# Attention and two feed-forward stages on one core: how many chunks of the first feed-forward run beside attention

## The chip, the core and the metric

The kernel runs on one core of a Trainium2 chip. What counts is the device time of one execution in microseconds (us). The kernel before took 1000.54 us in the median of three runs (1000.1 to 1000.61). Five engines work side by side: PE (matrix products), DVE and ACT (element work), POOL (element work), and SP, which here only issues transfers. PEld in the profile is PE's loading of stationary operands, which lies beside its products.

## What is computed

Three stages follow one another. Inputs are q, k, v of 4 batches, 8 heads, 576 positions and 64 dimensions; 2304 tokens of 512 features come out.

```
scores = q k^T / sqrt(D) - slope[h] * |i - j|, only where 0 <= i - j < 128
x      = softmax(scores) v            -> [2304, 512]
x      = ((x w_a) * (x w_b)) w_out    # feed-forward 1, hidden width 1536
h      = x w_in                       # feed-forward 2, hidden width 2048
g      = h where h >= 1, 0 where h <= -1, (h + 1)^2 / 4 between
out    = g w_out2                     -> [2304, 512]
```

The weights come as 64-bit floats. Each operand of a product is split into a high and a low part, and three products (high with high, high with low, low with high) stand for one.

## The kernel before, in words

**Tokens and chunks.** The tokens are cut into five blocks, 0 to 4, of 512, 512, 512, 512 and 256 tokens, and blocks 0 to 2 also into six halves of 256. The hidden width of feed-forward 1 is cut into 12 chunks of 128. One chunk takes three weights: a and b (into the hidden width, 12 matmuls each: 4 pieces of the 512 features times 3 products) and o (back to 512 features, 12 matmuls). So a chunk of a block costs 36 matmuls, whose length is the number of tokens, 512 or 256. Feed-forward 2 has 16 chunks of two weights.

**Attention.** The generator `attention()` lists 80 rounds of 128 queries for a pair of heads. Each is one step for the scores (L323 on PE, L329 on DVE, the exponential L333 on ACT, L338 on POOL, L339 on DVE, the division L342 or L344 on ACT or POOL), one for the transposition (L358 on PE, L360 copies it to `pt`), and one for the product with v for several rounds (L379 on PE), after which ACT writes `xh` (L392) and DVE `xl` (L393). That makes 192 steps. In the profile `xh` and copies through a helper stand as L149, copies on DVE as L151, and `xl` as L143.

**Feed-forward 1.** `gate()` runs the products with a and b (L523 to L525), copies a's result with ACT to `a_sb` (L563), multiplies it with b's on DVE (L568), and `parts()` splits it into `gh` (L545, ACT) and `gl` (L143). `down1_half()` (L596, 256 tokens) and `down1()` (L624 to L626) take these to accumulators. Where a half's chunks end, ACT and DVE copy the two accumulators to tiles `y`, and SP stores these in `x2p` in device memory (L607). When the block is taken up again, SP loads these sums back into `xsum` (L618), and later chunks are added to them.

**What sets the order.** `products()` lists turns: six halves with the first `N0` chunks each; then block 3 and block 4 with their first `N0` chunks, which wait for the whole of attention; then, as `TURN1` says, all blocks with chunks `N0` to `N1`; then, as `TURN2` says, with chunks `N1` to 12; then feed-forward 2. A half waits until attention has made its tokens. Every matmul group of three is a yield; at each, the main loop adds `PACE[turn]` to what it owes and takes one attention step per whole unit owed (L753 to L756). So `PACE` is the number of attention steps per three matmuls beside each turn; the last entry holds for all later turns. A scheduler then hoists what is ready, so that the recorded order is near but not equal to that.

**Weights.** `decode()` (L451) loads a weight (L459) and turns it into two 32-bit tiles with ACT, DVE and POOL (L472 to L490; L489 is ACT's last step). There are 15 slots for weights (`WP`) and 2 more once attention has ended (`W2`). A slot comes free when the last turn that uses its weight is recorded. Beside attention 15 weights, five chunks, are decoded.

**Where attention ends.** `step()` closes attention's pools and opens those of the later stage. One of these, tag `t` with two buffers, holds `a_sb`, and `y` of the half that is then under way.

Of the kernel before, what the change touches and what calls it, by code (L numbers as in the profile page):

```python
# [26 lines left out]
def attention_and_two_ffns(  # L27
# [45 lines left out]
    LORD = [['q', 0, 2, 'S'], ['k', 0, 2, 'A'], ['q', 2, 8, 'S'], ['k', 2, 8, 'A'], ['v', 0, 8, 'A']]  # L73
    LT = 3
    LV = 5
    N0 = [4, 5, 5, 5, 5]
    N1 = 9
    NDIAG = 2
    NHALF = 6
    PACE = [0.8, 0.8, 0.5, 0.5, 0.5, 0.5, 0.5, 0.5, 0.3]  # L80
    PT = 5
    PUMP = [2, 0]
    SB = 4
# [409 lines left out]
    def pump():  # L493
        if not waiting:
            return False
        free = [
            s for s in slots if len(s[2]) < s[1] or s[2][0] in retired
        ]
        if not free:
            return False  # L500

        pool, n, held = min(free, key=lambda s: order.index(s[2][0]) if len(s[2]) == s[1] and s[2][0] else -1)
        if len(held) == n:
            held.popleft()
        key = waiting.popleft()
        held.append(key)
        with tc.high_priority() if not later and HP(order.index(key)) else ExitStack():
            decode(key, pool)
        return True
# [170 lines left out]
    def products():  # L680
        behind = deque()

        def run(up, down, i, fs, x, n, final, lag):
# [9 lines left out]
        turns1 = [  # L693
            *((i, range(N0[t0 // TB])) for i, (t0, _) in enumerate(halves[:NHALF])),
            *((i, range(N0[i])) for i in range(NHALF // 2, len(blocks))),
            *((i, range(N0[i], N1)) for i in TURN1),
            *((i, range(N1, NF1)) for i in TURN2),
        ]
# [46 lines left out]
    for need in products():  # L745
        if need is not None:
            begun += 1
            while not later and (need > NT or not ready(need)):
                step()
                steps += 1  # L750
                if steps % PUMP[0] == PUMP[1]:
                    pump()
        owed += PACE[min(begun, len(PACE) - 1)]  # L753
        while owed >= 1.0:
# [32 lines left out]
```

## Time and profile before

| what | value |
|---|---|
| median of three runs | 1000.54 us |
| the profiled execution | 999.14 us, span of its instructions 997.4 us |
| PE busy | 967.6 us, 97% of the span |
| DVE, ACT, POOL busy | 612.7, 407.0, 178.2 us |
| stretch beside attention | 0 to about 245 us |
| TensorE's granted clock | 1.00 throughout |

The span is the time from the first to the last instruction that the profiler saw; 1.74 us of the execution lie around it. A turn's first L523 shows when it starts: the halves of block 0 at 29.0 us, of block 1 at 125.8, of block 2 at 205.7; block 3 at 265.5 and block 4 at 306.5; the turns of `TURN1` from 329.4, the last of them (block 4) at 466.9; block 0 of `TURN2` at 498.4; feed-forward 2 at 595.1. A busy time counts the modelled length of each matmul, and matmuls overlap; the pace of a run of matmuls is read from the distance of their starts.

### The profile page before, as it was taken

The page shows a single profiled execution, that of the slowest core. Times are in us where ns is not written, and L with a number is a line of the kernel's source. Part 1 is how long each engine was busy: PE and PEld are TensorE (multiplying, and loading weights), DVE is VectorE, ACT ScalarE, POOL GpSimd, SP SyncE. Part 2 cuts the span into 40 slices and gives each one's busy share as a digit, 9 for nine tenths or more (in the row PEclk, how much of TensorE's full clock was granted, in tenths as well). Part 3 has the DMA queues.
Part 4 walks back from the last instruction along what each step waited for, and adds up shares of the span by engine and source line. Part 5 has one row for each costly group of instructions (what it writes and reads, how often), then busy time and mean ns, then how long its engine had stood idle before and what let it go on. Part 6 is the DMA issues. An engine that isn't in the chain of part 4 may idle for free.

```text
span 997.4 us, 15119 instructions
## 1 busy us (share of the span) xinstructions
PE 967.6 (97%) x5624; PEld 836.9 (84%) x5624; DVE 612.7 (61%) x1354; ACT 407.0 (41%) x970; POOL 178.2 (18%) x289
## 2 busy tenths in 40 slices
PE   4889999999999999999999999999999999999998
PEld 3678899999989888888988887888888888888887
DVE  6999755553726993223995299634995446644443
ACT  4978767563314441112343245423552223322222
POOL 4777623221101100000222224000020000000001
PEclk9999999999999999999999999999999999999999
DMA  9777442311511331000231012100230000001111
GB/s 195 152 168 141 99 90 53 70 35 52 179 67 43 122 111 43 1 1 1 91 104 60 1 64 77 51 1 1 85 106 21 1 1 22 1 1 43 42 43 64
DMA packets 124121, 62.32 MB, mean 62 GB/s; under 512 B 95760, under 2 KB 116240, under 8 KB 123664
## 3 DMA queue, kind: packets, MB, share of 16 engines
q1 hardware_dynamic: 119824, 60.31, 22.6%
q10 hardware_dynamic: 4224, 1.05, 0.6%
q8 instruction: 44, 0.72, 0.3%
q14 instruction: 29, 0.24, 0.1%
HBM read 53.48 MB, written 7.86 MB: 62 GB/s over the span
## 4 chain that ended last, share of the span: by engine, by line
PE 84%; DVE 7%; DMA 3%; ACT 3%; issue 1%; POOL 1%; SPq 0%; DVEq 0%; ACTq 0%; POOLq 0%
PE mm L523 15%; PE mm L525 15%; PE mm L524 15%; PE acc L662 6%; PE acc L663 6%; PE acc L664 6%; PE acc L596 3%; PE acc L626 3%; PE acc L625 3%; PE acc L624 3%; PE ps_s L323 2%; PE ps_o L379 2%; PE ps_t L358 2%; DMA w<-in_moe_w_b_dram 1%; ACT s L333 1%
## 5 line engine op out<-in xcount | busy, mean ns | idle before, releaser
L523 PE MATMUL mm<-xh,wh 128*128 128x512 f32 (+1 forms) x912 | 321.2, 353 | 1.0 <-DVE c_sb L580 0.8
L525 PE MATMUL mm<-xh,wl 128*128 128x512 f32 (+1 forms) x912 | 314.2, 345 | 0.8 <-POOL wl L143 0.8
L524 PE MATMUL mm<-xl,wh 128*128 128x512 f32 (+1 forms) x912 | 314.5, 345 | 0.1
L523 PEld LDWEIGHTS mm<-xh,wh 128*128 128x128 f32 x912 | 172.2, 189 | 23.7 <-DVE c_sb L580 1.2
L524 PEld LDWEIGHTS mm<-xl,wh 128*128 128x128 f32 x912 | 172.4, 189 | 21.8 <-DVE xl L143 0.4
L525 PEld LDWEIGHTS mm<-xh,wl 128*128 128x128 f32 x912 | 172.1, 189 | 21.7 <-POOL wl L143 1.0
L579 ACT ACTIVATE c_sb<-c_sb,half 128x512 f32<-128x512 f32 (+1 forms) x80 | 54.5, 681 | 167.1 <-DVE c_sb L578 167.1
L662 PE MATMUL acc<-wh,gh 128*128 128x512 f32 x288 | 112.3, 390 | 0.0
L663 PE MATMUL acc<-wl,gh 128*128 128x512 f32 x288 | 112.2, 390 | 0.0
L664 PE MATMUL acc<-wh,gl 128*128 128x512 f32 x288 | 110.4, 390 | 0.0
L568 DVE TENSOR_TENSOR a_sb<-mm,a_sb 128x256 f32<-128x256 f32 (+1 forms) x74 | 40.2, 543 | 113.8 <-PE mm L525 103.5
L578 DVE TENSOR_SCALAR c_sb<-mm 128x512 f32<-128x512 f32 (+1 forms) x80 | 50.8, 635 | 82.5 <-PE mm L525 79.3
L143 POOL TENSOR_TENSOR gl<-c_sb,gh 128x256 fp32r<-128x256 f32 x16 | 14.4, 901 | 386.4 <-ACT gh L545 379.0
L143 POOL TENSOR_TENSOR gl<-a_sb,gh 128x256 fp32r<-128x256 f32 x40 | 36.6, 916 | 247.8 <-ACT gh L545 247.2
L580 DVE SCALAR_TENSOR_TENSOR c_sb<-mm,c_sb 128x512 f32<-128x512 f32 (+1 forms) x80 | 50.7, 635 | 39.0 <-ACT c_sb L579 39.0
L333 ACT ACTIVATE s<-s,nmax 128x192 f32<-128x192 f32 (+2 forms) x144 | 62.1, 433 | 23.9 <-DVE nmax L329 23.4
L563 ACT COPY a_sb<-mm 128x256 f32<-128x256 f32 (+1 forms) x74 | 34.5, 467 | 89.2 <-PE mm L525 81.9
L545 ACT CAST gh<-c_sb 128x512 fp32r<-128x512 f32 (+1 forms) x80 | 46.2, 579 | 55.8 <-DVE c_sb L580 46.2
L489 ACT CAST wh<-e 128x512 fp32r<-128x512 f32 x68 | 42.3, 622 | 64.1 <-DVE e L488 37.1
L472 ACT ACTIVATE e<-w 128x512 f32<-128x512 f32 x65 | 43.8, 674 | 58.5 <-DMA w<-in_moe_w_in_dram 14.2
L545 ACT CAST gh<-a_sb 128x256 fp32r<-128x256 f32 (+1 forms) x74 | 37.2, 502 | 74.3 <-DVE a_sb L568 74.0
L625 PE MATMUL acc<-gl,wh 128*128 128x512 f32 (+1 forms) x184 | 66.2, 362 | 0.2 <-DVE gl L143 0.2
(84 smaller groups left out, 1607.6 us busy)
## 6 DMA issues: line engine op xcount, KB each, us to landing
w<-in_moe_w_out_dram SPq DMA_DIRECT2D x28, 512.0 KB, 3.5
w<-in_moe_w_in_dram SPq DMA_DIRECT2D x16, 512.0 KB, 3.6
w<-in_moe_w_a_dram SPq DMA_DIRECT2D x12, 512.0 KB, 3.9
w<-in_moe_w_b_dram SPq DMA_DIRECT2D x12, 512.0 KB, 3.8
out_dram<-osum SPq DMA_DIRECT2D x18, 256.0 KB, 2.1
qraw<-in_q_dram SPq DMA_DIRECT2D x48, 72.0 KB, 2.7
kraw<-in_k_dram SPq DMA_DIRECT2D x48, 72.0 KB, 2.9
v<-in_v_dram SPq DMA_DIRECT2D x24, 128.0 KB, 2.9
```

Of the source, the lines that this page charges most:

```text
L143: eng.tensor_tensor(out_, a, hi.bitcast(F32), ALU.subtract)
L333: nc.scalar.activation(at(z, i), at(z, i), AF.Exp, bias=nmax[:, z : z + 1], scale=-1.0, accum_out=ssum[:, z : z + 1],)
L523: nc.tensor.matmul(ps, wh[:, cs], xh[:, c], start=(c == 0), stop=False)
L524: nc.tensor.matmul(ps, wh[:, cs], xl[:, c], start=False, stop=False)
L525: nc.tensor.matmul(ps, wl[:, cs], xh[:, c], start=False, stop=(c == NC - 1))
L545: nc.scalar.copy(hi[:, :n], t[:, :n])
L578: nc.vector.tensor_scalar(c_sb[:, :n], ph[:, :n], -1.0, None, ALU.max)
L579: nc.scalar.activation(c_sb[:, :n], c_sb[:, :n], AF.Square, bias=half, scale=0.5)
L625: nc.tensor.matmul(accs[c][:, :n], wh[:, cs], gl, start=False, stop=False)
L662: nc.tensor.matmul(accs[s], gh[:, ss], wh, start=begin, stop=False)
L663: nc.tensor.matmul(accs[s], gh[:, ss], wl, start=False, stop=False)
L664: nc.tensor.matmul(accs[s], gl[:, ss], wh, start=False, stop=end)
```

## The change

Three tables of numbers change, no other line. Every half, block 3 and block 4 take chunks 0 to 2 (`N0`) and no longer 0 to 3 or 0 to 4. `TURN1` takes chunks 3 to 7 of all five blocks (it was 5 to 8, and 4 to 8 for block 0), `TURN2` chunks 8 to 11 (it was 9 to 11). Beside all turns 0.8 attention steps are taken per three feed-forward matmuls; it was 0.8 beside the first two halves, 0.5 beside the next six turns and 0.3 later.

```diff
-    N0 = [4, 5, 5, 5, 5]
-    N1 = 9
+    N0 = [3, 3, 3, 3, 3]
+    N1 = 8
-    PACE = [0.8, 0.8, 0.5, 0.5, 0.5, 0.5, 0.5, 0.5, 0.3]
+    PACE = [0.8]
```

In numbers of the recorded order: matmuls of 512 tokens go from 2856 to 3036, those of 256 tokens from 1632 to 1272, and PE's changes between attention and feed-forward matmuls from 259 to 171. All 15 decodes of the first stage stay beside attention.

**PE, near the middle of the first batch's attention.** `ps_s`, `ps_t` and `ps_o` are attention's scores, transposes and values, `mm` and `acc` feed-forward 1. In a row before:

```order
L379 MATMUL ps_o_1749<-pt_1621,v1_146 64x128 x4
L379 MATMUL ps_o_1749<-pt_1647,v1_146 64x128 x4
L379 MATMUL ps_o_1749<-pt_1687,v1_146 64x64 x4
L323 MATMUL ps_s_1789<-kt_1583,diag0_128 128x64
L323 MATMUL ps_s_1789<-kt_1583,diag0_128 128x128
L358 MATMUL ps_t_1806<-ident_84,s2_138 128x128 x4
L525 MATMUL mm_1802<-xh0_106,wl_582 128x256
L323 MATMUL ps_s_1816<-kt_1583,diag0_128 128x192 x2
L523 MATMUL mm_1802<-xh0_106,wh_581 128x256
L524 MATMUL mm_1802<-xl0_107,wh_581 128x256
L525 MATMUL mm_1802<-xh0_106,wl_582 128x256
L523 MATMUL mm_1802<-xh0_106,wh_581 128x256
```

In a row now, at the same rounds of attention:

```order
L379 MATMUL ps_o_1740<-pt_1689,v1_146 64x64 x4
L323 MATMUL ps_s_1774<-kt_1584,diag0_128 128x64
L323 MATMUL ps_s_1774<-kt_1584,diag0_128 128x128
L358 MATMUL ps_t_1787<-ident_84,s2_138 128x128
L323 MATMUL ps_s_1794<-kt_1584,diag0_128 128x192 x2
L358 MATMUL ps_t_1787<-ident_84,s2_138 128x128 x3
L358 MATMUL ps_t_1807<-ident_84,s3_141 128x128 x4
L379 MATMUL ps_o_1814<-pt_1722,v2_148 64x128 x2
L379 MATMUL ps_o_1814<-pt_1738,v2_148 64x128 x4
L323 MATMUL ps_s_1827<-kt_1584,diag0_128 128x192 x2
L358 MATMUL ps_t_1843<-ident_84,s0_132 128x128 x2
L323 MATMUL ps_s_1851<-kt_1584,diag0_128 128x192 x2
```

Chunk 3 of the half before stood among these rounds (`mm_1802`, with `xh0`); now attention's rounds follow each other. Between `ps_o` of the round before (numbered 1656, now 1661) and that of the rounds after (1939, now 1903) 79 feed-forward matmuls stood in a row before and 12 stand now. Counted from the start to the end of this piece it was 294 and is 240.

**SP, where attention ends.** `xsum` are the loads of block 0's and 1's sums (1 MB each), `y` the store of a half's sums, `w64` weights that were not loaded beside attention. In a row before:

```order
L618 DMA xsum0_4581<-x2p_150 128x2048
L618 DMA xsum1_4891<-x2p_150 128x2048
L459 DMA w64_3672<-in_moe_w_a_dram 128x4x128
L459 DMA w64_3738<-in_moe_w_b_dram 128x4x128
L607 DMA x2p_150<-y_3732 128x512
L607 DMA x2p_150<-y_3735 128x512
```

And now:

```order
L618 DMA xsum0_3921<-x2p_150 128x2048
L618 DMA xsum1_4231<-x2p_150 128x2048
L607 DMA x2p_150<-y_3357 128x512
L607 DMA x2p_150<-y_3360 128x512
L459 DMA w64_3363<-in_moe_w_a_dram 128x4x128
L459 DMA w64_3425<-in_moe_w_b_dram 128x4x128
```

The two stores stood behind two weights, now directly behind the two loads; they belong to the fifth half before the change as after it.

**ACT, at the same place.** `xh4` is attention's last piece of x, `e` and `wh` steps of a decode. In a row before, from the first `a_sb` of the later stage:

```order
L563 COPY a_sb_3700<-mm_3687 128x256
L149 COPY y_3732<-acc_3308 128x512
L545 CAST gh_3716<-a_sb_3700 128x256
L472 ACTIVATE e_3676<-w64_3672 128x512
L472 ACTIVATE e_3742<-w64_3738 128x512
L563 COPY a_sb_3766<-mm_3753 128x256
L563 COPY a_sb_3813<-mm_3800 128x256
```

And now, from the fifth half's `y`:

```order
L149 COPY y_3357<-acc_3029 128x512
L149 CAST xh4_114<-ps_o_3298 128x256
L563 COPY a_sb_3391<-mm_3378 128x256
L563 COPY a_sb_3453<-mm_3440 128x256
L545 CAST gh_3407<-a_sb_3391 128x256
L545 CAST gh_3469<-a_sb_3453 128x256
L472 ACTIVATE e_3367<-w64_3363 128x512
```

Now `y_3357` takes the first of the two buffers of tag `t` in the later stage (its companion `y_3360` on DVE the second), and the next two `a_sb` take the same buffers again. On PE 60 feed-forward matmuls of halves are left behind the last of attention's; it was 195. Of the 60, the order has 12 for `acc_3411` and `acc_3412` (the two accumulators that `y_3357` and `y_3360` empty), 24 for `mm_3378` and `mm_3440`, then matmuls of block 3 (`mm_3485`, which takes the place in PSUM that `mm_3378` held until `a_sb_3391` is copied from it), and the other 24 among these.

## Rows read from the trace of the kernel before

**Rows 1.** The page's part 1: busy us (share of span), instructions.
```profile
PE 967.6 (97%) x5624; PEld 836.9 (84%) x5624; DVE 612.7 (61%) x1354; ACT 407.0 (41%) x970; POOL 178.2 (18%) x289
```

**Rows 2.** Windows: length, busy us (instructions) per engine, granted clock, DMA share, GB/s.
```profile
25.00:100.00 75.00, 66.40 (x568) 57.45 (x567) 71.14 (x233) 63.11 (x208) 57.18 (x85) 1.00 0.75 155
113.70:130.90 17.20, 17.20 (x171) 16.41 (x170) 10.59 (x47) 14.15 (x52) 7.41 (x20) 1.00 0.34 60
130.90:236.60 105.70, 105.70 (x973) 102.11 (x973) 53.34 (x223) 66.77 (x231) 30.71 (x84) 1.00 0.25 55
466.90:498.40 31.50, 31.50 (x253) 31.01 (x252) 28.29 (x54) 12.45 (x26) 6.20 (x6) 1.00 0.23 69
```

**Rows 3.** Timeline of PE, 256 tokens a matmul: start, us, line, operands.
```profile
247.06 0.28 PE L596 MATMUL acc<-gh,wh 128*128 128x256 f32 x1
...
247.66 0.28 PE L596 MATMUL acc<-gh,wl 128*128 128x256 f32 x1
```

**Rows 4.** Timeline of PE, 512 tokens a matmul.
```profile
401.61 0.39 PE L523 MATMUL mm<-xh,wh 128*128 128x512 f32 x1
...
402.75 0.39 PE L525 MATMUL mm<-xh,wl 128*128 128x512 f32 x1
```

**Rows 5.** Timeline of PE, entering feed-forward work from attention work.
```profile
131.33 0.36 PE L523 MATMUL mm<-xh,wh 128*128 128x256 f32 x1
131.53 0.28 PE L524 MATMUL mm<-xl,wh 128*128 128x256 f32 x1
...
132.29 0.41 PE L523 MATMUL mm<-xh,wh 128*128 128x256 f32 x1
132.54 0.28 PE L524 MATMUL mm<-xl,wh 128*128 128x256 f32 x1
```

**Rows 6.** Timeline of DVE at the two ends of the stretch.
```profile
113.67 0.42 DVE L143 TENSOR_TENSOR xl<-ps_o,xh 128x256 fp32r<-128x256 f32 x1
...
130.89 0.36 DVE L143 TENSOR_TENSOR xl<-ps_o,xh 128x192 fp32r<-128x192 f32 x1 [0.94 <-ACT xh L149]
```

**Rows 7.** Groups of ACT, 113.7 to 130.9: busy, mean ns, idle before, releasers.
```profile
L563 ACT COPY a_sb<-mm 128x256 f32<-128x256 f32 x3 | 1.1, 361 | 0.0
L545 ACT CAST gh<-a_sb 128x256 fp32r<-128x256 f32 x2 | 0.8, 388 | 0.0
```

**Rows 8.** Groups of PE, 130.9 to 236.6, one of each three alike.
```profile
L523 PE MATMUL mm<-xh,wh 128*128 128x256 f32 x106 | 35.5, 335 | 0.0
...
L596 PE MATMUL acc<-gh,wh 128*128 128x256 f32 x56 | 18.4, 329 | 0.0
```

**Rows 9.** Groups of ACT, 130.9 to 236.6.
```profile
L545 ACT CAST gh<-a_sb 128x256 fp32r<-128x256 f32 x14 | 5.6, 399 | 3.7 <-DVE a_sb L568 3.7
...
L563 ACT COPY a_sb<-mm 128x256 f32<-128x256 f32 x13 | 4.8, 371 | 3.8 <-PE mm L525 3.4 <-POOL ssum L338 0.3
...
L149 ACT COPY y<-acc 128x512 f32<-128x512 f32 x3 | 1.7, 572 | 0.0
```

**Rows 10.** Timeline of SP's queue where attention ends.
```profile
244.66 0.80 SPq L618 DMA_DIRECT2D xsum<-x2p  x2
248.02 0.38 SPq L459 DMA_DIRECT2D w<-in_moe_w_a_dram  x1
...
251.07 2.28 SPq L607 DMA_DIRECT2D x2p<-y  x2
```

**Rows 11.** DMA issues, whole span: KB each, median us to landing.
```profile
x2p<-y SPq DMA_DIRECT2D x12, 256.0 KB, 2.4
```

**Rows 12.** DMA issues from 244 to 258 us, columns as before.
```profile
xsum<-x2p SPq DMA_DIRECT2D x2, 1024.0 KB, 6.6
...
x2p<-y SPq DMA_DIRECT2D x2, 256.0 KB, 4.5
```

**Rows 13.** The decode's last ACT step, in 305 to 345 us.
```profile
L489 ACT CAST wh<-e x9: 620/622/628, 308.0 to 342.7; 128x512 fp32r<-128x512 f32 x9
```

## The prediction

> **What bounds the kernel now.** I read the page's part 1 first, then busy times by stretch, then timelines of single engines. PE is busy 97% of the span [rows 1], so the time is PE's work plus PE's few holes, and a change counts if it alters one of these. The stretches say where there are holes: from 25 to 100 us PE has 66.40 of 75 us and DVE 71.14; from 113.7 on PE has all of every stretch, at a granted clock of 1.00 in each [rows 2]. So beside attention PE is kept full from about 114 us by feed-forward work. The change takes a third of that work away, and the question is whether what is left still fills the holes.
>
> **Part 1, the matmuls themselves.** Ten half-chunks of 36 matmuls (28 beside attention become 18) leave, and five block-chunks of 36 come: 360 matmuls of 256 tokens for 180 of 512. Starts of the short ones lie 0.60 us apart over five of them, 0.120 us each [rows 3]; of the long ones 1.14 us over five, 0.228 us [rows 4]. 360 x 0.120 = 43.2 us against 180 x 0.228 = 41.0 us: a gain of 2.2 us.
>
> The Trainium skill ("TensorE: Matmul & The Clock Gate", section "Wait — 56ns, not 53.3ns?") speaks against most of it: a warm array starts a matmul every N / 2.4 GHz plus about 2.5 ns. By that the short one takes 109.2 ns and the long one 215.8 ns, both below the trace, and the gain would be 0.5 us, the sum 1.7 us higher.
>
> **Part 2, fewer changes between attention and feed-forward.** PE's order has 259 such changes and will have 171, so 44 entries into feed-forward work go. After an entry the second matmul starts 0.20 and 0.25 us after the first and not 0.12 [rows 5], 0.08 to 0.13 us more: 3.5 to 5.7 us in all. It may be that those starts only wait for attention's matmuls still in the array, which would cost nothing; I bound it by 0 and 5.7 and take the nearer row, 3.5 us gained.
>
> **Part 3, the stretch in which attention runs alone.** Block 0's second half now ends after chunk 2, and the third half cannot begin until attention has made block 1's first tokens. Between the two rounds of attention that end on DVE at 113.67 and 130.89 us [rows 6] PE will have 12 feed-forward matmuls and not 79. Counted to the stretch's end it will have done 240 and not 294: 54 x 0.120 = 6.5 us of PE's work still to do. Against it stands how much sooner the stretch ends. It took 17.2 us; without feed-forward work ACT decides. ACT was busy 14.15 us [rows 2], of which 1.1 + 0.8 us were feed-forward copies [rows 7] and about 0.4 us (one copy) stay: 12.7 us of work. That is the lower bound, if ACT never waits; at ACT's share of the old stretch, 14.15 / 17.2 = 82%, it takes 15.5 us; at worst it stays at 17.2, since the chain scores, DVE, ACT, POOL, DVE, ACT, transposition is as long as before. The loss is 6.5 - (17.2 - 12.7) = 2.0, 6.5 - 1.7 = 4.8, or 6.5 us. I take 4.8, as the share is a row of this very stretch. DVE's 10.59 us of 17.2 leave it behind ACT.
>
> **Part 4, the rest of attention.** From 130.9 to 236.6 us three times 106 and three times 56 [rows 8], 486 of 973 matmuls, are feed-forward. Of the 648 of all halves 240 will be done and 60 come after attention, so 348 remain. PE would need 105.7 - (486 - 348) x 0.120 = 89.1 us. ACT's 66.77 us fall by the copies of the work that goes, 28% of 5.6 + 4.8 + 1.7 us [rows 9], to 63.4, 71% of PE's time. Attention's chain gets shorter distances between its links (0.8 steps per three matmuls and not 0.5). Nothing excludes small holes: 0 to 3 us, I take 0.5, near PE's full row of before. That all of it were covered would mean 0. Were the whole rest to run with PE as in 25 to 100 us (89% busy), it would be 11 us; that is a rival.
>
> **Part 5, where attention ends.** Before, 195 feed-forward matmuls (23 us) stood behind attention's last, now 60 (7 us). At attention's end, call it t, pools change, and in SP's queue come the two 1 MB loads of `xsum`, issued together at 244.66 before [rows 10]. What is issued behind them is late: the store of `y` took 4.5 us to land where its median is 2.4 [rows 11, 12], though 6.4 us lay between the issues, which looks like a queue that hands out its bytes in order (2 MB of sums, 1 MB of weights, 0.5 MB of stores). Before, PE did not notice: 23 us of matmuls were there to do. Now `y_3357` and `y_3360`, copies of the fifth half, need the new pool, so they wait for t, though their sums are long done; `acc_3411`, PE's next matmul, waits for that copy: 0.57 us [rows 9] and the way there and back, 0.95 us together (estimate). Then 36 matmuls are free to run, 4.3 us, to t + 5.3. The next, `mm_3485`, needs `a_sb_3391`, whose buffer is `y_3357`'s, so it waits for the store to land. The store is issued about t + 1.2, behind the sums: these took 6.6 us to land [rows 12], and the store's own bytes come after them, so t + 7.8. ACT's copy, 0.4 us, and the signals follow. PE stands 3.0 us there, then some 0.6 us for the next `a_sb` behind the decodes that pile up on DVE, and 0.4 us while the short sequence drains: with the 0.95, 5.0 us. Bounds: 1.0 if the store overtakes the loads and lands in its median 2.4 us (t + 3.6, before PE needs it); 7 if the store takes two sums and both stores' time.
>
> **Part 6, the two last turns of feed-forward 1.** Five chunks' 15 weights fill the 15 slots, so at the passage from `TURN1` to `TURN2` only two weights of chunk 8 can be ready, and ten more are decoded while block 4 passes through both turns; it was seven. A decode takes (342.7 - 308.0) / 8 = 4.3 us [rows 13], ten 43 us; block 4 has 9 chunks, 324 x 0.120 = 39 us. Before: 8 chunks, 35 us, for 30 us of decodes, and PE was busy 31.50 of 31.50 us, DVE 28.29 [rows 2], with block 0's matmuls hoisted among it. So some 4 us are short and the hoisted block covers most. 0 to 4 us; 1.0, since before the row shows full cover. The passage to feed-forward 2 keeps its lookahead: 0.
>
> **Sum.** - 2.2 - 3.5 + 4.8 + 0.5 + 5.0 + 1.0 = + 5.6 us on the profiled execution's 999.14 us (span 997.4, 1.74 around it), 1004.7. That execution lies 1.40 us below the median of the runs; on the median the forecast is 1006.1, rounded 1006.0 us. With all gains at their largest and costs at their smallest, - 2.2 - 5.7 + 2.0 + 1.0 = - 4.9: 995.6; with the reverse, - 2.2 + 6.5 + 3 + 7 + 4 = + 18: 1018.8.
>
> **Rivals.**
> A, the other side: *the store is not behind the sums.* Place: `mm_3485`. If the store lands within 4.1 us of its issue (t + 1.2 to t + 5.3), PE never waits there and part 5 falls to 1.0; then the decodes alone remain, and with part 3 at ACT's own work, 2.0, the sum is - 2.2 - 3.5 + 2.0 + 0.5 + 1.0 + 1.0 = - 1.2 to - 4.9: about 997 us, faster. For it: sixteen DMA engines share the issues, and the store is only 256 KB. Against it: 4.5 us in the one place where this was seen.
> B, *attention becomes the bound to its end*: + 11 in place of 0.5, 1016 us. For it: 25 to 100 us, where PE is 89% busy beside the same pace of 0.8 steps. Against it: there 15 decodes load DVE to 95%, which are over by 114 us.
> C, *the last weights are late*: part 6's ten decodes are held by DVE, which was busy 90% of that stretch already; three more weights uncovered are 13 us, 1018 us. Against it: PE's full row, and block 0 can be hoisted further.
> D, *TensorE's clock falls at a new hole.* The granted clock was 1.00 in all stretches, those with holes of 11% too [rows 2]. If it fell to 1.2 GHz for 10 us of matmuls at t, these take 20: 1016 us. The same page of the Trainium skill (Part 1, "What's actually happening") has the clock gated down when the array has been idle; no row here shows it.
> E, *nothing happens*: the added holes and the saved matmuls cancel, 1000.5; it is the overlap of A and the forecast.
>
> **Chances.** The forecast, 1001 to 1011, 0.62; A 0.23 with E inside; B 0.07; C 0.05; D 0.03. What a measurement can tell from no change is 0.2%, 2 us: 998.5 to 1002.5. Of the forecast 0.08 lies within it and 0.54 above; of A 0.13 is faster, 0.10 the same; B to D are slower. Faster 0.13, same 0.18, slower 0.69. The range reaches from the middle of A to the start of B, 998.0 to 1013.0; the likeliest case's own is 1001 to 1011.
>
> **What would show it.** In the profile after: PE with holes between the rounds that ended at 113.67 and 130.89, and none from there to t; a wait of PE at L523 for ACT's `a_sb` (L563), about 3 us, some 5 us behind attention's last L379, and one at L596 for ACT's or DVE's `y`; the store of `y` taking over 6 us from issue to landing; PE's busy time lower by a few us. A store landing within 3 us proves A; holes all through 130 to 240 us prove B; a wait at L525 or L626 for `wl` before feed-forward 2 proves C. No new hole over 1 us anywhere would prove the forecast wrong.

## The result: 9 us slower

The changed kernel takes 1009.6 us in the median of its runs (1007.03 to 1010.62), the kernel before 1000.58 us: a ratio of 1.0082 (95% interval 1.0069 to 1.0095). The forecast was 1006.0 us, range 998.0 to 1013.0. The profiled execution took 1009.34 us, span 1007.6, 10.2 us more than before's span.

**Where PE waits now.** The longest sums of PE's waits (engine, line, what it waited for, us in all, times, longest):

```profile
PE ps_q L235 <- DMA qh<-in_q_dram: 9.5, 2, 6.3
PE ps_t L358 <- POOL s L344: 6.4, 7, 2.3
...
PE mm L523 <- ACT a_sb L563: 4.1, 1, 4.1
...
PE acc L596 <- ACT y L149: 1.1, 1, 1.1
```

In the kernel before:

```profile
PE ps_t L358 <- POOL s L344: 4.3, 5, 1.3
...
PE acc L596 <- DVE y L151: 0.6, 1, 0.6
...
PE mm L523 <- ACT a_sb L563: 0.2, 1, 0.2
```

The 4.1 us of `mm` (L523) for `a_sb` are new, and so is the wait of `acc` (L596) for a `y` at attention's end; the 0.6 us before lay at 106 us. By stretch (columns as in [rows 2]; the second is the stretch in which attention runs alone, the third the rest of attention, the fourth what follows the hole at t):

```profile
25.00:100.00 75.00, 68.94 (x587) 59.76 (x586) 70.78 (x226) 61.33 (x201) 56.61 (x83) 1.00 0.76 160
115.69:130.32 14.63, 13.17 (x127) 11.87 (x126) 11.01 (x51) 13.18 (x49) 5.83 (x17) 0.98 0.47 98
130.32:219.00 88.68, 88.68 (x834) 84.65 (x834) 51.23 (x218) 63.51 (x223) 28.00 (x81) 1.00 0.29 59
232.00:236.00 4.00, 3.46 (x9) 2.77 (x10) 2.13 (x5) 2.88 (x6) 1.43 (x2) 0.57 0.70 240
```

The granted clock was 1.00 before; now it is 0.98 in the second row and 0.57 in the fourth. The ends of the stretch on DVE, which answer to [rows 6]:

```profile
115.69 0.42 DVE L143 TENSOR_TENSOR xl<-ps_o,xh 128x256 fp32r<-128x256 f32 x1
...
130.32 0.35 DVE L143 TENSOR_TENSOR xl<-ps_o,xh 128x192 fp32r<-128x192 f32 x1
```

It took 14.6 us, before 17.2. The profile's chain of work through it (what released each step, or the step before it on its engine) runs over PE's own matmuls, but for one piece of 4 us, in which DVE transposes q and k of later rounds (`diag`, `kt`) and copies a `y` before POOL can divide and PE go on:

```profile
117.73 0.68 DVE diag L296
118.41 0.03 issue
118.44 0.78 DVE diag L296
119.22 0.03 issue
119.25 0.78 DVE kt L299
120.03 0.57 DVE y L151
...
120.84 0.43 POOL s L344
121.28 0.04 issue
121.32 0.33 PE ps_t L358
```

ACT does not stand in this chain. Where attention ends, SP's queue and DMA (as [rows 10, 12]):

```profile
222.91 0.82 SPq L618 DMA_DIRECT2D xsum<-x2p  x2
223.81 1.06 SPq L607 DMA_DIRECT2D x2p<-y  x2
```
```profile
xsum<-x2p SPq DMA_DIRECT2D x2, 1024.0 KB, 6.2
x2p<-y SPq DMA_DIRECT2D x2, 256.0 KB, 8.2
```

The store of `y` stood right behind the sums and took 8.2 us to land, before 4.5. ACT shows both waits: `y` is copied right after attention's last `xh`, and the next `a_sb` only when the store has landed:

```profile
222.81 0.21 ACT L149 CAST xh<-ps_o 128x64 fp32r<-128x64 f32 x1 [3.08 <-PE ps_o L379]
223.20 0.58 ACT L149 COPY y<-acc 128x512 f32<-128x512 f32 x1 [0.18 <-ACT xh L149]
...
232.12 0.75 ACT L563 COPY a_sb<-mm 128x256 f32<-128x256 f32 x2 [8.02 <-DMA x2p<-y]
```

PE's timeline there (the bracket is idle time before, and what ended it):

```profile
223.84 0.38 PE L596 MATMUL acc<-gh,wh 128*128 128x256 f32 x1 [1.07 <-ACT y L149]
...
228.13 0.28 PE L525 MATMUL mm<-xh,wl 128*128 128x256 f32 x1
232.54 0.80 PE L523 MATMUL mm<-xh,wh 128*128 128x512 f32 x1 [4.13 <-ACT a_sb L563]
233.13 0.63 PE L524 MATMUL mm<-xl,wh 128*128 128x512 f32 x1
233.56 0.63 PE L525 MATMUL mm<-xh,wl 128*128 128x512 f32 x1
...
235.27 0.56 PE L523 MATMUL mm<-xh,wh 128*128 128x512 f32 x1
235.66 0.39 PE L524 MATMUL mm<-xl,wh 128*128 128x512 f32 x1
235.89 0.40 PE L525 MATMUL mm<-xh,wl 128*128 128x512 f32 x1
```

PE stands for 4.13 us, then come matmuls of 512 tokens at a distance of 0.43 us, and from 235.66 on at 0.23: seven of them take 3.12 us (232.54 to 235.66) where 7 x 0.228 = 1.6 would do, 1.5 us more. That distance is the lower of the two clock levels, 1.2 GHz.

**Account.** At like places of attention I compare the times, and count each feed-forward matmul that is missing as 0.120 us:

| place (`xl` on DVE, where nothing else is said) | now, us | before, us | matmuls done, now / before | late by, us |
|---|---|---|---|---|
| the first | 30.1 | 29.1 | 1 / 1 | 1.1 |
| before the lone stretch | 99.8 | 96.8 | 202 / 164 | -1.6 |
| its start | 115.7 | 113.7 | 228 / 231 | 2.4 |
| its end | 130.3 | 130.9 | 244 / 294 | 5.4 |
| end of attention's last product on PE | 222.8 | 244.5 | 588 / 814 | 5.4 |
| the last | 224.1 | 245.5 | 590 / 821 | 6.4 |

The last `xl` has PE's wait of 1.07 us for `y` already behind it; attention's last product does not.

At equal work still to do, the new kernel is 9.5 us behind from 272 us on to the end of feed-forward 1, and 10.2 us from feed-forward 2's first turns to the end. With the 2.2 us that the longer matmuls save put back, that is: 1.1 at the start, 4.3 up to the end of the lone stretch (1.3 ahead of it, 3.0 in it), nothing in the rest of attention, 6.3 where attention ends, nothing between the two last turns of feed-forward 1, 0.8 at the entry to feed-forward 2, less 2.2 = 10.3. The 1.3 are the balance of a gain of 2.7 us up to 99.8 us, which the forecast did not have, and a loss of 4.0 from there to 115.7, more than half of it one wait of PE for POOL's division (2.3 us, to 111.7).

### The profile page after: what moved, and what is told of

Its sections match the earlier page's. It is cut to its first block, busy times and chain, and to the rows that moved or that the text cites. A ratio compares the mean times of both kernels' runs of the same rounds, so it can differ in the third digit from the quotient of the medians.

```text
span 1007.6 us, 14724 instructions
## 1 busy us (share of the span) xinstructions
PE 971.8 (96%) x5444; PEld 831.8 (83%) x5444; DVE 609.9 (61%) x1354; ACT 405.6 (40%) x960; POOL 170.1 (17%) x279
## 4 chain that ended last, share of the span: by engine, by line
PE 81%; DVE 5%; DMA 3%; issue 1%; ACT 1%; POOL 0%; DVEq 0%; ACTq 0%; SPq 0%; POOLq 0%
PE mm L523 15%; PE mm L524 14%; PE mm L525 14%; PE acc L664 6%; PE acc L663 6%; PE acc L662 6%; PE acc L624 4%; PE acc L625 4%; PE acc L626 4%; PE ps_s L323 3%; PE ps_o L379 2%; PE ps_t L358 2%; PE acc L596 2%; DMA x2p<-y 1%; DVE e L482 1%
## 5 line engine op out<-in xcount | busy, mean ns | idle before, releaser
L523 PE MATMUL mm<-xh,wh 128*128 128x512 f32 (+1 forms) x872 | 309.1, 356 | 4.2 <-ACT a_sb L563 4.1
L523 PEld LDWEIGHTS mm<-xh,wh 128*128 128x128 f32 x872 | 164.8, 189 | 28.1 <-ACT a_sb L563 4.6
L568 DVE TENSOR_TENSOR a_sb<-mm,a_sb 128x512 f32<-128x512 f32 (+1 forms) x69 | 39.3, 571 | 145.8 <-PE mm L525 137.8
L563 ACT COPY a_sb<-mm 128x512 f32<-128x512 f32 (+1 forms) x69 | 33.7, 489 | 108.8 <-PE mm L525 98.8
L625 PE MATMUL acc<-gl,wh 128*128 128x512 f32 (+1 forms) x204 | 73.7, 365 | 0.2 <-DVE gl L143 0.2
L626 PE MATMUL acc<-gh,wl 128*128 128x512 f32 (+1 forms) x204 | 73.5, 364 | 0.0
L545 ACT CAST gh<-a_sb 128x512 fp32r<-128x512 f32 (+1 forms) x69 | 36.3, 526 | 88.6 <-DVE a_sb L568 88.3
L624 PE MATMUL acc<-gh,wh 128*128 128x512 f32 (+1 forms) x204 | 69.9, 365 | 0.0
L143 POOL TENSOR_TENSOR gl<-a_sb,gh 128x256 fp32r<-128x256 f32 x30 | 27.1, 905 | 253.1 <-ACT gh L545 236.3
L323 PE MATMUL ps_s<-kt,diag 128*128 128x192 f32 (+2 forms) x288 | 63.1, 341 | 5.4 <-DVE kt L151 4.6
```

Source lines behind the costliest of these rows:

```text
L323: nc.tensor.matmul(ps[:, z, c : 3 * D], qd[:, i - q0 // D, :], kt[:, (i - 2) * D + c - k0 : (i + 1) * D - k0], start=True, stop=True,)
L523: nc.tensor.matmul(ps, wh[:, cs], xh[:, c], start=(c == 0), stop=False)
L545: nc.scalar.copy(hi[:, :n], t[:, :n])
L624: nc.tensor.matmul(accs[c][:, :n], wh[:, cs], gh, start=begin, stop=False)
L625: nc.tensor.matmul(accs[c][:, :n], wh[:, cs], gl, start=False, stop=False)
L626: nc.tensor.matmul(accs[c][:, :n], wl[:, cs], gh, start=False, stop=end)
```

## Experiments

Each ratio is to the kernel before, run beside it.

**e1: the stores of y on another queue.**
```diff
-                nc.sync.dma_start(
+                (nc.scalar if later else nc.sync).dma_start(
                     x2p[:, i, 2 * z : 2 * z + 2, :], ...
```


> The changed kernel, in which the stores of y that are issued after attention's end go out on ACT's queue and not on SP's behind the two loads of xsum. Theory (PE waited 4.1 us for a buffer whose store lay 8.2 us behind 2 MB of loads, and ran seven matmuls at 1.2 GHz after the hole): the store lands within about 5 us, PE's wait at mm_3485 falls below 1 us and the granted clock stays at 1.00 there; 1009.6 - 4.1 - 1.5 = about 1004, 1003 to 1006. Rival (the bytes are shared by all queues, or the wait is for the change of pools): the store still takes 7 us or more, 1008 to 1010.

1007.22 us, ratio 1.0066 (1.0051 to 1.0081). PE's waits and the DMA issues around t:

```profile
PE mm L523 <- ACT a_sb L563: 3.8, 1, 3.8
PE acc L596 <- ACT y L149: 1.1, 1, 1.1
```
```profile
xsum<-x2p SPq DMA_DIRECT2D x2, 1024.0 KB, 6.6
x2p<-y ACTq DMA_DIRECT2D x2, 256.0 KB, 8.1
```
```profile
228.00:230.00 2.00, 0.00 (x0) 0.00 (x0) 0.00 (x0) 0.00 (x0) 0.00 (x0) 1.00 1.00 387
```

The store was issued at once, on ACT's queue, and landed after 8.1 us all the same; PE waited 3.8 us, and the clock fell again. So it is not SP's order that delays the store. The last row (columns as in [rows 2]) has the DMA engines wholly busy while the store is under way, which speaks for the rival, that they are shared with the loads; that it is the 2 MB of sums, e5 shows. What e1 gained of its 2 us lies mostly ahead of t, where the edit touches nothing: its profiled execution has no fall of the clock at 112 us.

**e5: the loads of the sums later.**
```diff
+                nc.gpsimd.tensor_copy(sums[i][:, 0, 0, :1], g[0][:, :1].bitcast(F32))
                 nc.sync.dma_start(sums[i], x2p[:, 2 * i : 2 * i + nb])
```


> The changed kernel, in which each load of xsum follows a one-column POOL write that needs the first gh of its turn, so that the 2 MB no longer start at attention's end. Theory (PE's wait of 4 us at mm_3485 and the matmuls at 1.2 GHz behind it come from the stores of y sharing the DMA engines with these loads; another queue alone did not help): the store lands in 2 to 4 us, the wait is under 0.5 us, no fall of the clock there; ratio to before falls from 1.0082 by 0.005 to about 1.003, some 1003 to 1005 us. Rival (the wait comes from the change of pools, or is refilled by waits for the next weights): above 1.006.

1002.87 us, ratio 1.0021 (1.0009 to 1.0033). Around t:

```profile
PE acc L596 <- ACT y L149: 1.1, 1, 1.1
```
```profile
x2p<-y SPq DMA_DIRECT2D x2, 256.0 KB, 2.2
```

The store lands in 2.2 us, PE's wait for `a_sb` is gone, and so is the fall of the clock there. That is 0.006 of the 0.0082. By the account, attention's end now costs 0.6 us. The 1.1 us for `y` stay; that `y` waits there for the change of pools is read from the code and was not tested. The 12 runs lie between 999.98 and 1005.41 us, and this spread is not explained.

**e7: the same edit in the kernel before.**


> The kernel before with the loads of xsum later, nothing else. Theory (23 us of matmuls cover the loads there): no difference, ratio 0.999 to 1.001. Rival (the loads cost the kernel before too): 0.995 to 0.998.

999.72 us, ratio 0.9995 (0.9986 to 1.0003): no difference. So the loads became dear only with the change; that the 23 us of matmuls behind attention covered them before fits this.

**e2: block 0's halves keep four chunks.**
```diff
-    N0 = [3, 3, 3, 3, 3]
+    N0 = [4, 3, 3, 3, 3]
```


> The changed kernel with N0 = [4, 3, 3, 3, 3]: block 0's halves keep their fourth chunk, so feed-forward matmuls stand again in the stretch in which attention ran alone. Theory (that stretch cost 4.4 us, the pace of 0.8 later costs nothing): 1009.6 - 4.4 + 0.4 (72 short matmuls for 36 long ones) = about 1005.6, 1004 to 1007, with PE's holes between 100 and 130 us gone. Rival (the pace makes attention the bound for the whole rest): the holes only move later, 1009 to 1011.

1002.66 us, ratio 1.0025 (1.0015 to 1.0035), better than expected. From the same `xl` to the same `xl` as above (109.86 to 128.62 us) PE is full:

```profile
109.86:128.62 18.76, 18.76 (x183) 18.01 (x182) 11.75 (x49) 14.47 (x51) 6.00 (x18) 1.00 0.32 58
```

By the account above it is 1.4 us early two pieces of x later (133.6 us), where the changed kernel is 5.5 late (135.9): more than the lone stretch, since the 2.26 us hole ahead of it, at 109.5 to 111.7 us, is filled too. The hole behind t stayed: PE waits for `a_sb` for 0.9 us at t and 3.2 us up to 233.1. The clock behind it stays low for longer than in the changed kernel:

```profile
232.00:236.00 4.00, 2.91 (x7) 2.33 (x8) 2.10 (x4) 2.34 (x6) 2.87 (x4) 0.52 0.78 261
236.00:240.00 4.00, 4.00 (x13) 3.13 (x12) 3.45 (x7) 1.58 (x3) 1.67 (x2) 0.62 0.09 31
```

Fourteen matmuls of 512 tokens take 6.05 us there, 2.9 more than at 0.228 each.

**e6: both.**


> Both mends together: N0 = [4, 3, 3, 3, 3], and the loads of xsum later as in e5. Theory (the two holes are separate and are all that the change costs): 1.0025 - 0.005, a ratio of about 0.998, faster than the kernel before by some 2 us, which is the gain from 288 short matmuls against 144 long ones (1.8 us). Rival (the holes share a cause, or something else takes their place): 1.000 to 1.0025.

997.26 us, ratio 0.9967 (0.9955 to 0.9978): 3.3 parts in a thousand faster than the kernel before. The gains of e5 and e2 add up: 0.0082 - 0.0061 - 0.0057 = -0.0036. So the two costs are separate, and with both gone nothing of the loss is left. It is more than the 1.8 us that the longer matmuls give: two holes of the kernel before, 0.6 us at 106 us and 1.0 at 109, are not in e6. PE from 100 us to beyond attention's middle, and its wait around t:

```profile
100.00:130.00 30.00, 30.00 (x289) 28.71 (x288) 18.45 (x76) 22.64 (x80) 11.16 (x28) 1.00 0.44 86
130.00:220.00 90.00, 90.00 (x846) 85.79 (x845) 52.39 (x217) 62.61 (x220) 27.21 (x79) 1.00 0.29 62
```
```profile
PE mm L523 <- ACT a_sb L563: 0.9, 1, 0.9
```

**e3: the pace alone, in the kernel before.**
```diff
-    PACE = [0.8, 0.8, 0.5, 0.5, 0.5, 0.5, 0.5, 0.5, 0.3]
+    PACE = [0.8]
```


> The kernel before with the new pace of 0.8 for all turns, its chunks untouched; changes between attention and feed-forward on PE fall from 259 to 169, more feed-forward work is left behind attention. Theory (pace costs nothing as long as feed-forward work lies everywhere; a change between the kinds is worth 0 to 0.08 us for each of 45 entries): 997 to 1001. Rival (0.8 steps per three matmuls bind ACT and DVE for the rest of attention): 1004 to 1010.

1000.45 us, ratio 0.9997 (0.9988 to 1.0006). PE in the rest of attention:

```profile
130.00:220.00 90.00, 90.00 (x853) 86.06 (x852) 51.46 (x221) 63.58 (x223) 28.04 (x81) 1.00 0.29 59
```

So 0.8 steps bind nothing while feed-forward work lies beside (rival B is out), and 90 changes between attention and feed-forward fewer bring nothing that can be measured. The total alone could hide a gain, as PE has a new wait of 0.9 us for `a_sb` at t. But between two pieces of x, 136.6 to 207.1 us and in the kernel before 136.2 to 221.2, PE is full in both and changes 66 times where it changed 133 times; by the account e3 loses 0.5 us there, while 0.08 us for each of 33 entries would gain 2.6.

**e4: the chunks with the pace of before.** The diff is e3's the other way, in the changed kernel.


> The changed kernel's chunks (three beside attention, 3 to 7, 8 to 11) with the pace of before (0.8, 0.8, then 0.5 and 0.3). Theory (the chunks make the cost, since there is too little feed-forward work for attention's length): the work runs out before attention ends, so attention runs alone at its end as well; 1006 to 1013, not below the changed kernel by more than 3. Rival (the pace makes the cost): 1000 to 1003.

1005.6 us, ratio 1.0045 (1.0028 to 1.0063): neither. The lone stretch costs about as much as in the changed kernel (5.8 us late at its end, by the same account), but at attention's end PE waits for nothing longer than 0.4 us: by then the halves' work has run out and no `y` lies at the change of pools. The second hole needs the chunks and the pace together.

**e8 and e9: whose work sets the lone stretch.** In e5's kernel the second division of a round goes from ACT to POOL; in e8 for the first batch's second part, in e9 for the second batch.
```diff
-    E_N = ['PA', 'PA', 'PA', 'PA', ...
+    E_N = ['PA', 'PP', 'PA', 'PA', ...    # e8
+    E_N = ['PA', 'PA', 'PP', 'PP', ...    # e9
```


> The kernel of e5 (three chunks, loads of xsum later) with the second division of each round of the first batch's second part on POOL and not on ACT (E_N[1] = 'PP'). In the stretch in which attention runs alone this takes 7 x 0.45 us of ACT's 13.2 us away and adds as much to POOL's 5.8. Theory (ACT's work decides the stretch, as the prediction had it): the stretch of 14.6 us falls to about 12.5 and the time by 2 us, a ratio of about 1.000. Rival (the chain of dependent steps decides, POOL's division being its last link before PE's transposition): the stretch stays at 14 us or gets longer, the ratio stays at 1.002 or rises.

> The kernel of e5 with both divisions of each round of the second batch on POOL (E_N[2] and E_N[3] = 'PP'). The divisions in the 14.2 us in which attention runs alone are the second batch's (e8 changed the ones before them): 5 x 0.45 + 0.4 = 2.6 us of ACT's 13.05 go, POOL's 5.85 rise by as much. Theory (ACT's work decides that stretch): it falls to about 12 us, the ratio from 1.0021 to about 1.000. Rival (dependent steps decide): 14 us or more, the ratio 1.002 or above.

e8 took 1000.91 us, ratio 0.9996 (0.9986 to 1.0007); e9 1004.08 us, 1.0036 (1.0023 to 1.0048). e8 missed its aim: the divisions in the stretch belong to the second batch, and it kept its 14.3 us (113.06 to 127.35). It gained ahead of it, where in e5 POOL had kept PE's transposition waiting for 2.3 us and the clock then fell; in e8 this wait is 1.1 us and no clock falls. e9 hit the stretch, first e5's row, then e9's:

```profile
116.26:130.50 14.24, 12.78 (x126) 11.48 (x125) 11.01 (x51) 13.05 (x49) 5.85 (x17) 1.00 0.45 93
```
```profile
117.23:131.08 13.85, 13.02 (x128) 11.31 (x127) 11.01 (x50) 12.06 (x46) 8.09 (x22) 1.00 0.49 109
```

ACT has 1.0 us less to do, not 2.6 as expected, and the stretch is 0.4 us shorter; ACT is idle for 1.8 us of it. So ACT's work does not set it, which agrees with the chain shown above. That steps which wait for each other do, is argued: attention's 109 matmuls in the stretch take 12.7 of 14.6 us in the changed kernel, and 106 took 9.7 of 17.2 us before, each feed-forward one beside them (16 and 63 in these windows) counted at 0.120. Which of the steps would have to be shortened was not tested. The times of e9 and e5 cannot be told apart, as their intervals overlap.

**e10: e6 with e8's edit.**


> The kernel of e6 (four chunks for block 0, loads of xsum later) with E_N[1] = 'PP' as in e8. Theory (e8 gained by dropping a hole before 113 us that only three chunks leave open): no gain here, a ratio of 0.996 to 0.998. Rival (ACT was the bound there with four chunks too): 0.994 to 0.995.

1001.75 us, ratio 1.0012 (1.0003 to 1.0021): slower than e6, which neither side expected. Its account is 2 to 5 us late from 94 us on; which of the new order's waits does that was not followed up.

## Why the forecast was right, step by step

**Sign and size.** Forecast + 5.6, measured + 9.0. The two costs that carry it were both found where they were forecast; one gain did not exist, and one cost, the clock, had been put down as a rival.

**Part 1 (longer matmuls)** stands: 0.227 us from start to start for 512 tokens in the new kernel too (500.04, 500.26, 500.49). The rule of the Trainium skill ("TensorE: Matmul & The Clock Gate", "Wait — 56ns, not 53.3ns?") gives 215.8 ns; the trace does not agree. The 2.2 us follow from the distances in both traces.

**Part 2 (fewer changes, - 3.5 us) is the step that failed.** The late second matmul after an entry [rows 5] was read as a price of the change. e3 takes 90 changes away and gains 0.0003 (- 0.0006 to 0.0012), at most 1.2 us, and nothing in the stretch where PE is full with half the changes. The changed kernel shows the same: from the end of the lone stretch to attention's end it falls back by nothing and gains nothing. So the lower bound of 0 was the right one; its reason, matmuls of attention that are still in the array, was not tested. With 0 there the sum is + 9.1. That this is so near to 9.0 is luck: against the account it has 1.3 too little for part 5, 0.8 for feed-forward 2 and 1.1 for the start, and 2.0 too much for parts 3, 4 and 6.

**Part 3 (the lone stretch, + 4.8)** measured + 4.3 with the 1.1 us of the start left out, in 14.6 us where 15.5 were taken. That the place was right is shown by e2; that the size fits is in part luck, since the stretch is 0.9 us shorter than taken and 1.3 us were lost ahead of it, which the sum did not have: there lies the hole of 2.26 us up to 111.7 us, with the clock at 0.59 from 112 to 116 us behind it. ACT as the reason was wrong: it is not in the chain, and e9 took work from it with little effect.

**Part 4 (+ 0.5)** measured 0, PE without idle time. **Part 6 (+ 1.0)** measured 0: the delay stays at 9.4 to 9.6 us over both turns, so the ten decodes were covered. Its working has a slip: before, block 4 had 7 chunks left and not 8, 252 matmuls or 30 us, as the 253 matmuls in [rows 2] show; the decodes had been covered without room to spare. The entry to feed-forward 2, put at 0, costs 0.8; e4, with the same chunks, loses 0.2 there, and the cause stays open.

**Part 5 (attention's end, + 5.0)** measured + 6.3: 1.07 for `y` (0.95 forecast), 4.13 for `a_sb` (3.0), as the store landed at t + 9.2 and not t + 7.8, and 1.5 for the clock, which the sum did not have; 0.4 of these 6.7 do not show in the account. The 1.0 us that the forecast added for what comes late afterwards was not found. The chain of waits was right; the reason for the late store, a queue that serves in order, was wrong (e1).

**Rival D happened** in small: 1.5 us behind the hole at 232.5 us, and at other places in some executions (20 to 24 us and 112 to 116 us in the profiled one, neither in e1's). The granted clock was 0.57 behind the 4.13 us hole. The Trainium skill's rule that an idle array is clocked down ("TensorE: Matmul & The Clock Gate", Part 1, "What's actually happening") agrees with it. That falls differ from execution to execution does not explain why the changed kernel's runs spread over 3.6 us: two of the four, both with a mean granted clock of 0.996, took 1007.03 and 1009.86 us. Rival A's condition, a store that lands within 4.1 us, is what e5 makes true, with its gain: part 5 falls to 0.6, where A had 1.0.

The first `xl` came 1.1 us late; in e7, whose first stage is the kernel before's, it came 1.6 us late, so such a delay needs no change.

## What to carry to other kernels

Work that is moved out of a stage may have been the cover for two things that cost nothing before: a stretch of steps that cannot fill PE alone, and a transfer that happened to start there. Ask of each stage that loses work what PE has to do while the next tokens are made, and what a buffer at the seam between stages waits for. Both could be mended on their own (e2, e5), and with them the same idea is a gain (e6).

## What the runs showed of the hardware

Two stores of 256 KB, issued 0.9 us behind 2 MB of loads, took 8.2 us to land from the same queue and 8.1 us from another; without the loads they took 2.2 us (the changed kernel, e1, e5). Behind a hole of 4.13 us TensorE ran at 1.2 GHz for 3.1 us, behind one of 3.16 us (e2) for 6.0 us, although it had been busy for over 4 us up to each hole. The hole cost 1.5 us more than its length in the one and 2.9 us more in the other.
